# Retention with a two-layer MLP on one core: loads of tiles 18 to 23 in one run, v scaled by GpSimd alone, another order of late tasks

## The chip, the cores and the metric

The kernel runs on one core of one Trainium2 chip. The metric is the device time of one execution in microseconds (us). A core has engines that run side by side, each through its own list of instructions in order, and that wait for each other by semaphores: TensorE (PE; its weight loads are shown apart as PEld), VectorE (DVE), ScalarE (ACT), GpSimd (POOL) and SyncE (SP), which here only issues transfers. Transfers (DMA) are issued by SP, ACT and POOL and carried out by 16 DMA engines.

## The reference

Inputs q, k and v have the shape 4 x 8 x 768 x 64 (batch, heads, sequence, head width). The first half is a recurrent retention, the second a layer norm with a two-layer MLP and a residual:

```python
gamma = 1.0 - 2.0 ** (-5.0 - np.arange(H))
for t in range(S):
    state = gamma * state + np.einsum('bhd,bhe->bhde', k[:, :, t], v[:, :, t])
    y[:, :, t] = scale * np.einsum('bhd,bhde->bhe', q[:, :, t], state)
...
xn = (x - mu) / np.sqrt(var + 1e-06) * g_ln
ch = np.maximum(xn @ w_ch1, 0.0) @ w_ch2
return x + ch
```

x is y with its heads side by side, 3072 rows of 512; w_ch1 is 512 x 2048, w_ch2 is 2048 x 512. Inputs and output are fp32.

## The kernel before

The 3072 rows are cut into 24 tiles of 128 tokens. Tiles 0 to 3 are the first chunk of each batch; tiles 4 to 8 are chunks 1 to 5 of batch 0, 9 to 13 of batch 1, 14 to 18 of batch 2, 19 to 23 of batch 3. All matmuls are in bf16. Inside a chunk the recurrence is a masked product of scores; between chunks of a batch a state is carried on.

For each late tile (from tile 7 on) the steps are: POOL loads k, q and v (`k`, `q`, `v`, line 361, three DMAs of 128 KB with a cast to bf16) into ring buffers, eight slots for q with k and nine for v; SP transposes q and k together by DMA (`tr`, line 404); DVE scales the transposed q (`eq`, line 410); PE makes the scores of a pair of tiles in the four PSUM banks X0 to X3 and adds the carried state's part to the banks Y0 and Y1 (`vis`, lines 419 and 425); DVE applies mask and decay (`am`, line 432); PE multiplies by v (`py`, line 447). v scaled per head (`vg`) is made either by ACT in eight instructions, one for each head (line 478), or by POOL in one (line 481); PE multiplies it with k onto the bank PD, which sums over the chunks of a batch (`pd`, line 489), and DVE or ACT turns PD into the next state (`pb`, lines 500 and 504). There are three slots for scaled v, so a scaling waits until PE has used the one three chunks earlier.

The norm follows: DVE takes mean and variance (`bn`, lines 455 and 456), ACT the root (`sr`, line 586), DVE the reciprocal and the shift (`rt`, `nb`, lines 595 and 590), ACT copies y (`xc`, line 471) and normalizes it (`xg`, line 599), SP transposes it by DMA into `xnt` (`ex`, line 524). The first layer takes tiles in groups: eight of one tile, four of two (groups 8 to 11: tiles 8 and 9, up to 14 and 15), two of four (groups 12 and 13). `m8_4` is the block of group 8 that starts at hidden column block 4; it goes to one of the banks X0 to X3 (line 549), and ACT or DVE applies the relu into `h` and frees the bank (`r`, lines 560 and 562). Groups 12 and 13 use seven products instead of eight for a 2 x 2 block scheme (`f`, `fs`, `fo`, `fq`, `fr`, lines 670 to 711). The second layer runs tile by tile for tiles 0 to 7 (`z`, line 567) and in pairs with the seven products for the others (`s`, `sa`, `o`, lines 736, 725 and 750), and the result is stored (`st`, line 582).

**What sets the order.** Nothing is scheduled at run time: the list `ORDER` names every task in the order in which it is emitted, and each engine runs its own share of that list in order. `/A` behind a name puts it on ACT, `/D` or nothing on DVE (for `vg`, nothing means POOL), and the names behind `//` are the PSUM banks. A task on an engine that waits thus holds everything that stands behind it on that engine.

**The gates.** `gk17` and the like (`gate`, line 390) copy one element of a loaded buffer to `scrap` on POOL. They compute nothing: the copy waits for the landing of that load, and so POOL's later loads are issued only when it has landed. Landings are told on eight semaphores that POOL's loads use in turn (DMASW0 to DMASW7 in the rows below).

Of the kernel before, what the change touches and what calls it, by code (L numbers as in the profile page):

```python
# [52 lines left out]
am11a ad5 py10 r6_4/A py11 v14 pd11 m7_4//X1 bn11 pb12/A gq14 gk13 z6_0//M wg3/D st1/A gk15 r7_4/A
v13 pd12 bn10 m8_14//X0 sr11 xc11a q15 xc10b rt11 m8_8//X1 pb13 xc11b xc10a v15 sr10 nb11 z6_1 rt10
xg11b nb10 rs6 eq12 xg10b r8_14/A gk14 tr14 z6_2 wg1/D r8_8/A z6_3 v16 xg10a eq13 xg11a ex11/S
vis12//X0,X1,X2,X3 ad6 pd2 gv14 am13b vg14/ z7_0//M ex10/S pb14/A am12a m8_12//X3 gv13 am13a gq15
tr15 m8_2//X0 am12b tm4 py13 r8_2/A py12 z7_1 xc13a k16 xc13b bn12 r8_12/A pd14 m8_0//X0 vg15/A q16
bn13 z7_2 k17 sr13 m8_6//X1 xc12a rt13 q17 eq14 sr12 sq7 nb13 z7_3 rt12 pb15 xg13a v17 xg13b xc12b
m8_10//X2 ex13/S rs7 nb12 r8_6/A ad7 gv16 vg16/ r8_0/A m8_4//X1 r8_10/A gv15 xg12b k18 tm3 m9_8//X0
xg12a r8_4/A ex12/S pd15 st2/A eq15 s8_1//M r9_8/A sa8_1 st7/A gk17 vis14//X0,X1,X2,X3 pb16/A sa8_2  # L60
s8_5 gq17 am14a tr16 am14b pd16 gv17 m9_0//X0 gk16 am15a py14 am15b m9_4//X1 gk18 q20 py15 st3/A
m9_2//X2 tr17 bn15 r9_0/A k20 r9_4/A m9_6//X3 sa8_4 vg3/A q18 m10_2//X0 bn14 r9_6/A m9_12//X1 sa8_3
r9_2/A q19 sr14 s8_2//X3 sr15 r10_2/A o8_1 k19 xc15b vg17/A rt14 rt15 s8_6 nb15 pb17 gq20 s8_3 o8_2
r9_12/A eq16 xg15a m9_10//X0 xg15b o8_3 xc15a eq17 xc14b gq18 tr18 m9_14//X1 xc14a o8_4 v19 r9_10/A
nb14 wm3 xg14b s8_7 xg14a gq16 r9_14/A pd17 o8_5 vis16//X0,X1,X2,X3 pb18/A sa10_1 v18 tr19 s8_4
am16b gk19 am16a pd3 m10_4//X1 v20 ex15/S am17a py16 gq19 o8_6 st5/A m10_6//X0 ex14/S am17b st4/A
pb19/A bn16 s10_1//M tr20 py17 sa10_3 sr16 m10_10//X2 r10_6/A sa10_2 st6/A s10_5 rt16 r10_10/A
sa10_4 xc16b m10_12//X0 bn17 r10_4/A gv18 v21 m10_8//X1 wm1 sr17 gv19 xc17b k21 xc17a s10_2//X2
xc16a r10_8/A gk20 rt17 nb16 nb17 o10_1 m10_14//X3 r10_12/A vg20/ xg16b xg16a s10_6 xg17a q21 eq18
r10_14/A o10_2 s10_3 xg17b eq19 v22 vg19/A vis18//X0,X1,X2,X3 o10_3 o10_4 pd19 am19a s10_7 am18a  # L70
gk21 m10_0//X2 am18b q22 am19b m11_6//X0 k22 r10_0/A o10_5 pb20/A py18 sa12_1 q23 py19 s10_4 bn18
r11_6/A tr21 vg22/ pd20 m11_14//X0 o10_6 sr18 rt18 ex16/S vg21/ nb18 m11_0//X1 bn19 r11_14/A gv20
xc19b s12_1//M ex17/S gq21 eq20 r11_0/A wm2 sr19 s12_5 xg18b k23 xc18b pb21/A rt19 sa12_2 m11_8//X0
v23 nb19 sa12_3 xg19a m11_4//X1 xg18a o12_1 xg19b r11_8/A s12_2//X2 ex19/S sa12_4 xc19a r11_4/A wm4
pd21 s12_6 xc18a ex18/S pb22/A o12_2 s12_3 eq21 pd22 vis20//X0,X1,X2,X3 o12_3 tr22 o12_4 s12_7 am20a
pb23/A am21a f12_1_1//X0 am20b f12_0_1//PD m11_2//X2 xt12_1 fs12_0_1 am21b fs12_1_1 f12_0_5//X1
xt12_2 py20 tr23 o12_5 fs12_0_5 f12_0_2//X3 xt12_3 f12_0_6 r11_2/A fo12_0_1 py21 fs12_0_2 f12_0_3
bn20 f12_1_6 xc21a s12_4 st8/A fo12_0_2 fs12_1_2 f12_1_5//X2 xc21b xt12_4 xc20b f12_1_7 bn21
fs12_1_5 m11_10//X1 sr20 xc20a fo12_1_3 sr21 f12_1_3 r11_10/A rt20 rt21 m11_12//X3 nb20 nb21 eq23
xg20a eq22 f12_1_4 r11_12/A o12_6 f12_1_2//X1 fo12_1_2 xg20b f12_0_7 xg21b xg21a fo12_1_1 s14_1//M  # L80
fq12_1 ex21/S fo12_0_3 st13/A vis22//X0,X1,X2,X3 sa14_1 ex20/S f12_0_4 am23a s14_5 am23b f12_2_1//X2
am22b f12_3_1//X3 st9/A am22a py23 fs12_2_1 f12_2_5//X1 sa14_2 fs12_3_1 py22 f12_2_6 fs12_2_5 sa14_3
f12_3_6 fs12_2_2 sa14_4 f12_2_3 xc23a f12_3_5//X0 fs12_3_2 fo12_2_2 f12_2_7 fq12_0 o14_1 f12_3_7
st10/A f12_3_2//X1 xc22b bn22 fr12_0_1/A s14_6 fs12_3_5 bn23 s14_3 sr22 s14_2//PD rt22 sr23 o14_3
rt23 nb22 o14_4 f12_3_3 xg22b nb23 xg22a fo12_3_3 s14_7 xg23a ex22/S xc22a fo12_3_2 xg23b f12_3_4
xc23b o14_2 fr12_1_1/A f12_2_2//X0 o14_5 ex23/S f13_0_1//Y0 fr12_1_2/D fo12_2_1 s14_4 fo12_3_1
fs13_0_1 f13_0_2//X0 fo12_2_3 st11/A f13_2_1//X1 fq12_3 fo13_0_1 f13_1_1//Y1 fr12_2_1/A f12_2_4
# [763 lines left out]
```

## Time and profile before

| | |
|---|---|
| median of 3 runs | 207.77 us (207.06 to 208.0) |
| the profiled execution | 207.04 us |
| its span, first to last instruction | 205.2 us |
| granted TensorE clock | 0.998 |
| TensorE busy | 194.9 us, 95% |
| VectorE busy | 165.0 us, 80% |
| ScalarE busy | 126.0 us, 61% |
| GpSimd busy | 94.2 us, 46% |
| DMA queue of POOL's loads | 77024 packets, 13.37 MB |

Busy times are those of the engine's own instructions; issuing a DMA counts on POOL (some 0.9 us for each load) and not on SP or ACT. In groups of rows the columns are: line, engine, operation, output and inputs, shapes and count, then busy time, mean ns of one, and the idle time before them with what ended it. In timelines: start, duration, engine, line, operation, count, and in brackets the idle time of the engine just before, with what ended it. The end of the program is a run of PE products, a last addition and a store, in both versions the same.

### The profile page before, as it was taken

To read this page: it belongs to the slowest core of one execution; us is meant where nothing else is said; L and a number is where in the kernel's file an instruction comes from. 1 tells how busy PE (TensorE), PEld (TensorE's weight loads), DVE (VectorE), ACT (ScalarE), POOL (GpSimd) and SP (SyncE) were. 2 spreads that over 40 slices of the span, in tenths; PEclk is the share of its full clock that TensorE was granted. 3 is DMA by queue.
4 is the path that set the end of the run, shared out by engine and by line. 5 is a ranking of instruction groups with operands and counts; after the bars stand their busy time and mean duration, and the time that the engine had idled before them with its cause. 6 is when DMAs were issued, how large, how long until landed. Compare 5 with 4: busy or idle time off the path is not lost.

```text
span 205.2 us, 5787 instructions
## 1 busy us (share of the span) xinstructions
PE 194.9 (95%) x2292; PEld 159.3 (78%) x2303; DVE 165.0 (80%) x388; ACT 126.0 (61%) x316; POOL 94.2 (46%) x139
## 2 busy tenths in 40 slices
PE   7998999999999999998997998999999999999992
PEld 3568999897546576666986987988989888888881
DVE  6687899587258799967787996988988998879961
ACT  6376644641426998589499496895949896543000
POOL 8997593694597398695806198600000000000000
PEclk9999999999999999999999999999999999999999
DMA  8999999999999999999999999988142140102224
GB/s 128 173 182 180 159 194 167 175 181 156 159 111 166 147 118 168 169 155 209 179 133 107 205 190 104 137 75 126 56 144 65 26 131 0 51 3 102 104 82 177
DMA packets 110477, 27.16 MB, mean 132 GB/s; under 512 B 103153, under 2 KB 107505, under 8 KB 110450
## 3 DMA queue, kind: packets, MB, share of 16 engines
q0 software_dynamic: 77024, 13.37, 87.9%
q1 hardware_dynamic: 28770, 6.86, 24.4%
q10 hardware_dynamic: 4656, 6.56, 9.5%
q8 instruction: 18, 0.29, 0.6%
q14 instruction: 9, 0.07, 0.1%
HBM read 27.30 MB, written 6.29 MB: 164 GB/s over the span
## 4 chain that ended last, share of the span: by engine, by line
PE 37%; ACT 13%; DVE 3%; issue 2%; ACTq 0%; DVEq 0%
PE M L736 11%; PE X L670 8%; PE Y L736 5%; PE X L549 5%; ACT xn L599 3%; ACT vg L478 3%; ACT h L560 3%; PE Y L670 2%; PE PD L670 2%; ACT x_all L471 1%; PE X L736 1%; PE X L419 1%; PE Y L447 1%; ACT state L500 1%; PE PD L736 1%
## 5 line engine op out<-in xcount | busy, mean ns | idle before, releaser
L549 PE MATMUL X<-xnt,w 128*128 128x128 bf16 (+1 forms) x768 | 64.0, 237 | 0.9 <-ACT h L560 0.9
L549 PEld LDWEIGHTS <-w 128*128 128x128 bf16 x768 | 53.9, 98 | 6.0 <-issue 1.3
L560 ACT ACTIVATE h<-X 128x512 bf16<-128x512 f32 x57 | 33.5, 607 | 17.8 <-PE X L549 17.6
L432 DVE TENSOR_TENSOR asb<-X,mask 128x512 bf16<-128x512 f32 x48 | 30.3, 682 | 1.7 <-PE X L419 1.4
L736 PEld LDWEIGHTS <-h 128*128 128x128 bf16 x256 | 24.7, 98 | 3.3 <-issue 0.4
L567 PE MATMUL M<-w,h 128*128 128x512 bf16 x87 | 22.1, 379 | 0.5 <-issue 0.2
L567 PEld LDWEIGHTS <-h 128*128 128x128 bf16 x128 | 11.8, 98 | 11.7
L736 PEld LDWEIGHTS <-sum 128*128 128x128 bf16 x192 | 18.7, 98 | 2.6 <-issue 0.4
L455 DVE BATCH_NORM_STATS2 bns<-Y 128x6 f32<-128x256 f32 (+1 forms) x39 | 16.3, 451 | 5.2 <-PE Y L447 3.8
L471 ACT CAST x_all<-Y 128x256 bf16<-128x256 f32 (+1 forms) x39 | 14.8, 410 | 8.4 <-DVE xn L465 7.8
L361 POOL DMA_DIRECT2D v<-in_v_dram x20 | 17.8, 890 | 3.2 <-DMA w<-in_moe_w_ch_dram 2.2
L599 ACT ACTIVATE xn<-Y,shift,rstd 128x256 bf16<-128x256 f32 x32 | 16.7, 580 | 1.5 <-DVE shift L590 0.8
L361 POOL DMA_DIRECT2D qk<-in_k_dram x17 | 15.4, 906 | 1.0 <-issue 1.0
L361 POOL DMA_DIRECT2D qk<-in_q_dram x17 | 15.0, 889 | 1.1 <-issue 1.1
L500 ACT ACTIVATE state<-PD,gch 128x128 bf16<-128x128 f32 x40 | 11.7, 401 | 4.7 <-PE PD L489 3.6
L481 POOL TENSOR_TENSOR vg<-v,vsc 128x512 bf16<-128x512 bf16 x11 | 11.4, 1042 | 6.5 <-DMA v<-in_v_dram 6.5
L750 DVE TENSOR_TENSOR osb<-M,x_all 128x256 f32<-128x256 f32 (+1 forms) x18 | 9.1, 506 | 5.5 <-PE M L736 5.5
L390 POOL COPY scrap<-qk 1x1 bf16<-1x1 bf16 x28 | 8.9, 320 | 10.0 <-DMA qk<-in_q_dram 6.1
L736 PE MATMUL M<-early,sum 128*128 128x256 bf16 x96 | 12.4, 273 | 0.2 <-DVE osb L750 0.2
L736 PE MATMUL M<-w,h 128*128 128x256 bf16 x96 | 12.4, 273 | 0.0
L711 ACT ACTIVATE h<-h 128x1024 bf16<-128x1024 bf16 (+1 forms) x10 | 8.5, 862 | 5.5 <-DVE h L697 5.5
L725 DVE TENSOR_TENSOR sum<-h,sum 128x1024 bf16<-128x1024 bf16 x16 | 10.9, 681 | 0.1
(164 smaller groups left out, 375.6 us busy)
## 6 DMA issues: line engine op xcount, KB each, us to landing
out_dram<-osb ACTq DMA_DIRECT2D x23, 256.0 KB, 2.3
w<-in_moe_w_ch_dram POOLq DMA_DIRECT2D x8, 512.0 KB, 8.5
v<-in_v_dram POOLq DMA_DIRECT2D x20, 128.0 KB, 6.5
qk<-in_k_dram POOLq DMA_DIRECT2D x17, 128.0 KB, 6.6
qk<-in_q_dram POOLq DMA_DIRECT2D x17, 128.0 KB, 6.3
early<-in_q_dram POOLq DMA_DIRECT2D x6, 128.0 KB, 7.6
mid<-in_k_dram POOLq DMA_DIRECT2D x3, 128.0 KB, 6.8
mid<-in_v_dram POOLq DMA_DIRECT2D x3, 128.0 KB, 7.5
```

Source lines behind the costliest of these rows:

```text
L361: nc.gpsimd.dma_start(out=dst, in_=tok[kind][TILES[t]])
L432: nc.vector.tensor_tensor(out=slot(asb, t)[:, :, par, :], in0=bank(("pa", t, par)).rearrange("p (i t) -> p i t", t=P), in1=mask.rearrange( ...
L455: nc.vector.bn_stats(out=bns[:, t, i, :], in_=x)
L471: nc.scalar.copy(out=dst, in_=src)
L481: nc.gpsimd.tensor_tensor(out=slot(vgs, chunk(t)), in0=v_of(t), in1=vsc[:, c, :].unsqueeze(2).to_broadcast([P, H, D]), op=ALU.mult)
L500: nc.scalar.activation(out=slot(state, chunk(t) - 1)[:, i, :], in_=pd[:, i, :], func=AF.Copy, scale=gch[:, c - 1, i:i + 1])
L549: nc.tensor.matmul(bank(("mm", g, ho))[:, j * n * P:(j + 1) * n * P], lhsT=w1[:, ko, (ho + j) * P:(ho + j + 1) * P], rhs=x[:, x0:x0 + n, k ...
L560: nc.scalar.activation(out=dst, in_=src, func=AF.Relu)
L567: nc.tensor.matmul(bank(("m2", t)), lhsT=slot(h1, t // 4)[:, ho, t % 4 * P:(t % 4 + 1) * P], rhs=w2[:, ho, :], start=(ho == 0), stop=(ho = ...
L599: nc.scalar.activation(out=heads(slot(xns, t))[:, :, half], in_=split(y_of(t, half)), func=AF.Identity, bias=shift[:, t:t + 1], scale=rstd ...
L670: nc.tensor.matmul(f_bank(g, j, i)[:, n * w:(n + 1) * w], lhsT=f_left(i, ko)[:, (nb * j + n) * P:(nb * j + n + 1) * P], rhs=f_right(g, i)[ ...
L736: nc.tensor.matmul(product(t, i), lhsT=left(t, i)[:, ho, :], rhs=right[i][:, ho, :], start=(ho == 0 and i in (1, 2)), stop=(ho == HK - 1), ...
```

## The change

The list `ORDER` is replaced from the scores of tiles 8 and 9 on (some 62 us into the span), and nothing else. Its first lines:

```diff
-z2_3 ad0 tr10 gq10 z3_0//M v12 gk11 st0/A ad2 z3_1 tr11 eq8 q13 vis8//X2,X1,X3,X0 wg0/A tm1 z3_2
-am8a am8b z3_3 am9b pd9 am9a m7_12//X1 pb10/A gv10 gv11 ad3 q12 py8 py9 vg10/A z4_0//M bn9 z4_1 bn8
+z2_3 ad0 tr10 gq10 z3_0//M v12 gk11 st0/A ad2 z3_1 tr11 eq8 q13 vis8//X2,X1,X3,X0 wg0/A tm1 pd9 am8b
+z3_2 pb10/A am8a z3_3 am9a am9b m7_12//X1 gv10 q12 ad3 py8 py9 vg10/ z4_0//M bn9 z4_1 gv11 vg11/ bn8
...
```

Three things differ. Fifteen gates are gone: those of k of tiles 16 to 21, of q of tiles 16, 17, 18 and 20, of v of tiles 15, 16, 18, 19 and 20. The scaling of v of tiles 10, 11, 15, 3, 17 and 19, which was on ACT, is on POOL, so that none is left on ACT. And the late tasks stand in another order, with other banks; a few small tasks change between ACT and DVE (the first layer's weight scalings `wg1` and `wg2` and the states of tiles 14 and 17 change places; of the relus `fr` five go to DVE and three to ACT). No other task is added or removed: PE has the same 4605 rows.

On POOL, the place where the loads of tiles 18 to 20 begin. Before (`v_106` to `v_108` are slots of the v ring, `qk` the ring of q and k; what a row waits for stands in brackets, and a DMA row without brackets has had its waits fulfilled by rows ahead of it):

```order
L361 DMA qk_111<-in_q_dram 128x8x64 [waits DMAHW7_49]
L361 DMA qk_111<-in_k_dram 128x8x64
L361 DMA qk_111<-in_q_dram 128x8x64
L361 DMA qk_111<-in_q_dram 128x8x64 [waits DMAHW3_49,DMASW0_49]
L361 DMA qk_111<-in_k_dram 128x8x64
L390 COPY scrap_71<-qk_111 1x1 [waits DMASW5_49,Pool_49]
L390 COPY scrap_71<-qk_111 1x1 [waits DMASW7_49,Pool_49]
L361 DMA v6_108<-in_v_dram 128x8x64
L390 COPY scrap_71<-qk_111 1x1 [waits Pool_49]
L361 DMA v5_107<-in_v_dram 128x8x64
L390 COPY scrap_71<-qk_111 1x1 [waits DMASW1_49,Pool_49]
L361 DMA v7_109<-in_v_dram 128x8x64
```

and after the change, from v of tile 17 (`v4_106`) on:

```order
L361 DMA v4_106<-in_v_dram 128x8x64
L361 DMA qk_111<-in_q_dram 128x8x64 [waits DMAHW2_49]
L361 DMA qk_111<-in_k_dram 128x8x64
L361 DMA qk_111<-in_q_dram 128x8x64 [waits DMAHW3_49,DMASW6_49]
L481 TENSOR_TENSOR vg1_118<-v3_105,vsc_84 128x512 [waits PE_49]
L361 DMA v5_107<-in_v_dram 128x8x64 [waits DMASW7_49]
L361 DMA qk_111<-in_k_dram 128x8x64 [waits DMASW0_49]
L361 DMA v6_108<-in_v_dram 128x8x64 [waits DMASW1_49]
L390 COPY scrap_71<-v4_106 1x1 [waits DMASW3_49,Pool_49]
L361 DMA qk_111<-in_q_dram 128x8x64 [waits DMAHW7_49,DMASW2_49]
L361 DMA qk_111<-in_k_dram 128x8x64
L361 DMA qk_111<-in_k_dram 128x8x64 [waits DMAHW0_49,DMASW4_49]
```

The copies between the loads, which wait for landings, are gone but one, and the loads themselves carry the wait for the semaphore that a load eight places earlier uses; a scaling of v (`vg1_118`, tile 16) stands among them.

On ACT, between the first-layer blocks of group 9 (`h10`) ahead of the scores of tiles 16 and 17. Before, with the scalings of v of tiles 3 (`mid`) and 17 (`v4`):

```order
L560 ACTIVATE h10_129<-X0_61 128x2x256
L560 ACTIVATE h10_129<-X1_62 128x2x256
L478 ACTIVATE vg0_117<-mid_101,vsc_84 128x64 x8
L560 ACTIVATE h10_129<-X3_64 128x2x256
L560 ACTIVATE h10_129<-X2_63 128x2x256
L586 ACTIVATE rstd_91<-mv_90,epsb_76 128x1 x2
L560 ACTIVATE h11_130<-X0_61 128x2x256
L471 CAST x_all_96<-Y1_66 128x4x64
L478 ACTIVATE vg2_119<-v4_106,vsc_84 128x64 x8
L560 ACTIVATE h10_129<-X1_62 128x2x256
```

and after it, from an evacuation of the same group on:

```order
L560 ACTIVATE h10_129<-X0_61 128x2x256
L586 ACTIVATE rstd_91<-mv_90,epsb_76 128x1 x2
L560 ACTIVATE h10_129<-X3_64 128x2x256
L560 ACTIVATE h10_129<-X2_63 128x2x256
L560 ACTIVATE h10_129<-X1_62 128x2x256
L471 CAST x_all_96<-Y0_65 128x4x64
L560 ACTIVATE h11_130<-X0_61 128x2x256
L599 ACTIVATE xn3_125<-Y0_65,shift_92,rstd_91 128x4x64
L599 ACTIVATE xn2_124<-Y1_66,shift_92,rstd_91 128x4x64
```

The two times eight instructions of L478 are gone; evacuations (L560) and the norm's steps follow each other.

On SP, which issues all transposes: `tr` are q and k of a tile (L404), `xnt0` the normalized tiles 12 to 15, of which `xn2` is tile 14 and `xn3` tile 15, and `xnt1` tiles 16 to 19. The piece of the difference:

```order
 L524 DMA_TRANSPOSE xnt0_126<-xn1_123 128x4x128
-L524 DMA_TRANSPOSE xnt0_126<-xn0_122 128x4x128
+L404 DMA_TRANSPOSE tr_112<-qk_111 128x8x128 x2
+L524 DMA_TRANSPOSE xnt0_126<-xn3_125 128x4x128
 L404 DMA_TRANSPOSE tr_112<-qk_111 128x8x128 x4
-L524 DMA_TRANSPOSE xnt0_126<-xn3_125 128x4x128
 L524 DMA_TRANSPOSE xnt0_126<-xn2_124 128x4x128
-L404 DMA_TRANSPOSE tr_112<-qk_111 128x8x128 x2
+L404 DMA_TRANSPOSE tr_112<-qk_111 128x8x128
+L524 DMA_TRANSPOSE xnt1_127<-xn1_123 128x4x128
 L524 DMA_TRANSPOSE xnt1_127<-xn0_122 128x4x128
```

Tile 15's transpose (`xn3`) now stands ahead of those of q and k of tiles 18 to 21, and tile 14's (`xn2`) stays behind all four, where before only those of tiles 18 and 19 were ahead of both; behind tile 14 comes one `tr` (tile 23) in place of two.

More of the change, by code (lines that the diff above doesn't have):

```diff
@@ L53 @@
[L53 to L87, printed above, removed]
@@ new lines @@
+m10_8//X1 am16a pb19/A tr21 v23 bn17 m10_10//X3 r10_8/A vg20/ py16 ex14/S sr17 s10_1//M r10_10/A
+rt17 nb17 vg21/ bn16 s10_5 tr23 xc16a st6/A sr16 m10_4//X0 xc16b rt16 nb16 wm1 xg16a s10_2//X1
+r10_4/A xg16b m10_12//X3 xc17b o10_1 st7/A xg17b sa10_4 s10_6 xg17a r10_6/A ex17/S eq19 r10_12/A
+s10_3 eq18 xc17a o10_2 ex16/S vis18//X0,X1,X2,X3 o10_3 o10_4 pd19 am19b s10_7 pb20/A vg22/ am19a
+m10_0//X3 o10_5 gq21 am18a py19 r10_0/A s10_4 am18b sa12_1 pd20 py18 pb21/A m11_6//X0 o10_6 bn19
+m11_4//X1 bn18 sr19 pd21 s12_1//M r11_4/A sa12_2 sr18 s12_5 rt19 sa12_4 m11_14//X1 rt18 eq20 nb18
@@ new lines @@
+nb19 wm2 m11_8//X2 xg19a xg19b r11_6/A ex19/S m11_0//X3 xg18a o12_1 xg18b xc18a sa12_3 s12_2//X0
+xc19a ex18/S xc19b eq21 r11_14/A s12_6 o12_2 r11_0/A tr22 wm4 xc18b s12_3 r11_8/A pb22/A
+vis20//X0,X1,X2,X3 o12_3 o12_4 pd22 am20b s12_7 pb23/A am20a f12_1_1//X1 xt12_1 f12_0_2//X0 am21b
+fs12_1_1 py20 f12_0_1//PD xt12_2 st8/A am21a f12_1_5//X3 fs12_0_1 f12_1_6 xt12_3 py21 fo12_0_1
+fs12_1_2 f12_0_6 xt12_4 f12_0_5//X2 fs12_1_5 bn21 m11_2//X0 st11/A fs12_0_2 f12_1_3 bn20 fs12_0_5
+f12_1_7 r11_2/A f12_0_3 fo12_1_2 sr20 m11_10//X0 sr21 xc20b rt21 rt20 nb20 fo12_1_3 f12_0_7
@@ new lines @@
+f12_1_2//X3 nb21 o12_5 xg21b f12_1_4 fo12_0_3 xg20b r11_10/A s12_4 fo12_0_2 xg21a xg20a eq23
+m11_12//X0 xc21b ex20/S xc20a o12_6 fq12_1 fo12_1_1 f12_0_4 r11_12/A s14_1//M eq22 ex21/S xc21a
+sa14_1 fq12_0 vis22//X0,X1,X2,X3 sa14_2 f12_3_1//PD am23b s14_5 am23a f12_2_1//X3 am22b py23 st9/A
+f12_3_2//X2 am22a fs12_3_1 f12_3_5//X1 sa14_4 fs12_2_1 py22 f12_3_6 fs12_3_5 bn22 f12_2_6 xc22a
+s14_2//X0 fs12_3_2 bn23 sr22 fs12_2_2 f12_3_7 f12_3_3 xc22b o14_1 sr23 f12_2_7 rt22 o14_2 s14_6 rt23
+nb22 fo12_3_2 xg22a xg22b s14_3 nb23 xc23b fo12_3_3 ex22/S xg23b xg23a f12_2_5//X0 fo12_3_1 xc23a
@@ new lines @@
+s16_1//PD sa16_1 st15/A fr12_3_2/A f13_0_4 sa16_2 fs13_2_5 f13_2_7 fo13_1_2 s16_5 fs13_3_2
+f13_3_2//X0 fq13_0 o16_1 f13_2_3 fo13_3_1 f13_3_5//X2 f13_3_7 fo13_2_2 fs13_3_5 s16_2//X0 sa16_4
+s16_6 fo13_3_3 sa16_3 s16_3 fo13_2_3 f13_1_4 fr13_2_2/D f13_3_4 sa18_1 fq13_1 f13_2_4 o16_3 fq13_3
+s18_1//Y1 sa18_2 fr13_3_2/A o16_4 st14/A s18_5 o16_2 fr13_0_1/A sa18_4 f13_3_3 fr13_1_1/A fr13_2_1/D
+s16_7 fq13_2 s18_2//X0 o16_5 o18_1 s16_4 fo13_3_2 s18_6 fr13_3_1/D o16_6 s18_3 sa20_1 st17/A
+fr13_0_2/A sa20_2 s20_1//Y0 st16/A o18_3 s20_5 sa18_3 fr13_1_2/D s22_1//M o20_1 o18_4 s20_2//X1
@@ L100 @@
+sa20_4 s20_6 sa22_1 sa20_3 s22_5 o18_2 s22_2//X2 o22_1 sa22_2 s20_3 sa22_3 s18_7 o20_3 sa22_4 s22_6
+o18_5 o20_4 s22_3 s18_4 o22_3 o22_4 s20_7 o20_2 o22_2 s22_7 st22/A o20_5 o18_6 s20_4 st19/A o22_5
+st18/A s22_4 st20/A o20_6 st23b/A st21/A o22_6 st23a/A
 """.split()
```

38 lines of the change are left out of this document (23 added, 15 removed).

## The prediction

> **What bounds the kernel now.** I read the busy times first, then what TensorE (PE) waits for, then the rows at each wait.
>
> ```profile
> PE 194.9 (95%) x2292; PEld 159.3 (78%) x2303; DVE 165.0 (80%) x388; ACT 126.0 (61%) x316; POOL 94.2 (46%) x139
> PE X L419 <- ACT h L560: 1.2, 1, 1.2
> PE X L549 <- ACT h L560: 0.9, 1, 0.9
> PE PD L489 <- ACT vg L478: 0.5, 2, 0.3
> PE X L419 <- ACT h L702: 0.4, 1, 0.4
> PE M L736 <- DVE osb L750: 0.2, 1, 0.2
> PE PD L489 <- ACT state L500: 0.2, 1, 0.2
> ```
>
> The first row is the page's, the others are PE's waits from 62 us on (total, times, longest), without one of 0.2 us that names no engine. The order differs only from the scores of tiles 8 and 9 on, which PE starts at about 62 us; the matmuls are the same before and after, so the change can win PE's waits behind 62 us and no more. These seven waits are 3.4 us. The ends of matmuls are modelled, so each wait is longer than its row:
>
> ```profile
> L736 PE MATMUL M<-w,h 128*128 128x256 bf16 x96 | 12.4, 273 | 0.0
> 158.60 1.75 PE M L736 x16
> ```
>
> A 256-column matmul is shown 273 ns long (group row), but sixteen in a run take 1.75 us (chain), 109 ns each. The last one before a gap thus covers 0.16 us of it; seven gaps add 1.1 us. The **ceiling** of the gain is 4.5 us of PE's time.
>
> ```profile
> 93.89 1.91 PE L549 MATMUL X<-xnt,w 128*128 128x256 bf16 x16 [0.94 <-ACT h L560]
> 111.51 0.60 PE L419 MATMUL X<-trq,tr 64*128 64x128 bf16 x15 [1.18 <-ACT h L560]
> 122.12 1.03 PE L736 MATMUL M<-early,sum 128*128 128x256 bf16 x8 [0.24 <-DVE osb L750]
> 123.96 0.62 PE L419 MATMUL X<-trq,tr 64*128 64x128 bf16 x16
> 125.78 0.22 PE L489 MATMUL PD<-vg,qk 128*128 128x128 bf16 x1 [0.26 <-ACT vg L478]
> 138.48 0.38 PE L489 MATMUL PD<-vg,qk 128*128 128x128 bf16 x4 [0.22 <-ACT state L500]
> 151.50 0.62 PE L419 MATMUL X<-trq,tr 64*128 64x128 bf16 x16 [0.35 <-ACT h L702]
> ```
>
> These timeline rows place the waits (the scores of tiles 18 and 19, at 123.96, have none and are quoted for later); a twin of that at 125.78, 0.25 us, stands just before it. Five of the seven name ScalarE (ACT). What holds it there:
>
> ```profile
> 88.58 2.01 ACT L478 ACTIVATE vg<-v,vsc 128x64 bf16<-128x64 bf16 x8
> 101.63 1.77 ACT vg L478 x7
> 105.46 1.91 ACT vg L478 x8
> 123.72 2.02 ACT L478 ACTIVATE vg<-v,vsc 128x64 bf16<-128x64 bf16 x8
> sum 90.00, ACT 12.08; mean ACT 2.42
> ```
>
> Rows one and four are timeline, two and three the chain that ended last, five the sum of line 478 over windows from 62 to 152 us. Scaling v for one tile takes ACT eight instructions and 1.9 us; six tiles make 12.1 us. Each stands ahead of the evacuations (L560) that free score banks for PE.
>
> **The change, part by part.** *Scaling v on GpSimd (POOL).*
>
> ```profile
> L481 POOL TENSOR_TENSOR vg<-v,vsc 128x512 bf16<-128x512 bf16 x11 | 11.4, 1042 | 6.5 <-DMA v<-in_v_dram 6.5
> ```
>
> 48 ACT instructions go, POOL gets 6 x 1.04 = 6.3 us. At 93.89 ACT loses 1.9 us ahead of the wait, against 0.94 + 0.16; at 111.51 it loses 1.77 + 1.91 = 3.7 us, against 1.18 + 0.16; at 125.31 and 125.78 the waited-for work itself leaves, if POOL has it ready. I take these four waits as gone: 0.94 + 1.18 + 0.25 + 0.26 + 4 x 0.16 = 3.3 us. *Order:* the product on PD of tile 22 (138.48) is moved behind the scores of tiles 20 and 21, and one block (f12_0_4) ahead of the scores of tiles 22 and 23 is now followed by another product, so those two waits, 0.22 + 0.35 + 0.32 = 0.9 us, lose their cause too. The one at 122.12 belongs to POOL, below. The new order has its own tight places (four banks X0 to X3, each reused after two to four products). Unknown from the trace: at best nothing, at worst such waits as it shows at 93.89, 1.1 us; I take 0.4, as in the 138.48 row.
>
> *The port.* What VectorE (DVE) meets beside POOL's scaling:
>
> ```profile
> 120.33 1.13 DVE L590 SCALAR_TENSOR_TENSOR shift<-mv,rstd 128x1 f32<-128x1 f32 x2
> 120.34 1.03 POOL L481 TENSOR_TENSOR vg<-v,vsc 128x512 bf16<-128x512 bf16 x1
> 121.39 0.68 DVE L750 TENSOR_TENSOR osb<-M,x_all 128x512 f32<-128x512 f32 x1
> 90.89 1.02 DVE L410 TENSOR_TENSOR trq<-tr,qsc 128x512 bf16<-128x512 bf16 x1
> 128.41 0.95 DVE L725 TENSOR_TENSOR sum<-h 128x1024 bf16<-128x1024 bf16 x1 [0.75 <-ACT h L560]
> L590 DVE SCALAR_TENSOR_TENSOR shift<-mv,rstd 128x1 f32<-128x1 f32 x16 | 3.2, 209 | 0.1
> L410 DVE TENSOR_TENSOR trq<-tr,qsc 128x512 bf16<-128x512 bf16 x17 | 7.5, 447 | 3.1 <-DMA tr<-qk 3.0
> L725 DVE TENSOR_TENSOR sum<-h 128x1024 bf16<-128x1024 bf16 x8 | 5.7, 718 | 2.9 <-ACT h L560 2.9
> ```
>
> A 0.2 us shift pair took 1.13 us and ended with POOL's scaling; L410 took 1.02 instead of 0.45, L725 0.95 instead of 0.72, all beside it. Together about 1.7 us, over the seven scalings that POOL has behind 62 us: 0.25 us each. Six more cost DVE 1.5 us. The first case reached PE: the late osb at 121.39 is the wait at 122.12, 0.40 with its 0.16, so 0.4 of 0.9 us came through. I take 0.6 us of PE time for the six, within 0 (DVE has slack: 85% busy from 62 to 139 us) and 1.5 (all comes through), and keep the old 0.4 at 122.12 as not won. The Trainium skill speaks against the change here: in "SBUF — State Buffer", section "SBUF: two separate sides", the two engines share a port pair as an exclusive lock, and the second to come blocks fully. The trace agrees with that direction in the three rows above; what the rule would cost at its hardest is a rival below.
>
> *Loads.* Fifteen one-element copies (L390) go, with their waits.
>
> ```profile
> 105.22 0.18 POOL L390 COPY scrap<-qk 1x1 bf16<-1x1 bf16 x1 [3.21 <-DMA qk<-in_q_dram]
> 108.05 0.18 POOL L390 COPY scrap<-qk 1x1 bf16<-1x1 bf16 x1 [2.65 <-DMA qk<-in_q_dram]
> 117.17 0.57 POOL L390 COPY scrap<-v 1x1 bf16<-1x1 bf16 x1 [5.58 <-DMA v<-in_v_dram]
> v<-in_v_dram POOLq DMA_DIRECT2D x20, 128.0 KB, 6.5
> ```
>
> These three hold POOL for 11.4 us, yet no PE wait names a load. So I price earlier loads at nothing in themselves; what they buy is that PE, some 3 us earlier by then, still finds its tiles there. The landing waits are not all gone: by the order's rows a load now itself waits for the one eight before it, and a scaling queued behind such a load waits with it. That of tile 19 stands behind the loads of v and k of tile 22. PE needs it right behind the scores of tiles 18 and 19, 123.96 - 3 + 1 = 122 us.
>
> ```profile
> 89.58 0.91 POOL L361 DMA_DIRECT2D v<-in_v_dram  x1
> 130.52 0.89 POOL L361 DMA_DIRECT2D v<-in_v_dram  x1
> ```
>
> From v of tile 17 (first row) to v of tile 23 (second) before issued 18 more loads in 41 us, 2.3 us each with POOL's waits; issue alone is 0.9 us. I take 2.0. Three more scalings (3.1 us) stand ahead of the first row's load now, so it goes out at 90 to 93 us. The load that k of tile 22 waits for is the ninth behind it and lands by 90 + 18 + 6.5 = 114.5 to 117.5 us, so scaling 19 is ready by 118 to 121: hidden, by 1 to 4 us; without that cover each microsecond late is one of PE's.
>
> *SyncE (SP).* The transposes of q and k of tiles 18 to 21 and then that of normalized tile 14 now stand in a row.
>
> ```profile
> 110.88 5.01 SPq L524 DMA_TRANSPOSE xnt<-xn  x2
> 116.06 10.45 SPq L404 DMA_TRANSPOSE tr<-qk  x2
> DMA to landing us min/median/max: 2.4/3.4/8.8
> ```
>
> Before, tile 14 (second of the pair at 110.88) went out ahead of tiles 20 and 21; now behind both, so it needs q of tile 21, the tenth load behind v 17: 90 + 20 + 6.5 = 116.5 to 119.5 us. Then 1.3 us of issue and 3.4 (median of xnt, last row) to 8.8 us to land: 121 to 124, at worst 130. PE wants it for m11_6, three blocks of 0.87 us (8 of the 109 ns products) and some 0.7 us of small products behind 122: at 126. I take no wait; the bounds are 0 and 4 us, and the far end is a rival.
>
> *Sum:* won 3.3 + 0.9 = 4.2; paid 0.4 + 0.6 = 1.0; net 3.2 us. The profiled execution took 207.04 us (span 205.2 and 1.8 around it): 203.8 us. The median shown, 207.77, is 0.7 above it, and the same scatter may lie on the new one; it stands in the range, not in the forecast.
>
> **Rivals.** *Transposes late.* Loads now run beside all transposes, where POOL's waits left gaps before. For it: with a landing of 8.8 us, the longest quoted, tile 14 is up to 4 us late, and the scores of tiles 16 and 17 (111.51 before, 110 now) lose their spare time too. Against it: their scores, just as close in before, waited for ACT and never for a transpose. Price 1 to 2.5 us: 205.5. The Trainium skill, "DMA: Bandwidth & Descriptors", section "Queues, rings and completion order", has each engine go round its queues packet by packet, so that more loads waiting in one queue need not slow another; no run here shows that yet.
>
> *Slower by late loads.* q of tile 21 lands as late as before, since transfers and not POOL's waits set the pace. Before, SP's pair from 116.06, whose second is tile 21, ended at 126.5. Then tile 14 goes out at 126.5 and lands at 130 to 135, and PE, in order, stands at m11_6 from 126: 4 to 9 us lost against 3.2 won, 210.3 in the middle. It turns slower from a landing of q 21 at about 124. Against it: 11.4 us of POOL's waits leave the queue ahead of that load.
>
> *Slower by the port.* Each of the six scalings holds a DVE instruction for its whole length and PE waits for that instruction: 6 x 1.04 = 6.2 us, against 4.2 - 0.4 won: 209.4 us. The rows speak for one such hold in seven. This is the rule of "SBUF — State Buffer" in the Trainium skill at its hardest.
>
> *No effect.* ACT's freed time is eaten by the new order's bank waits, DVE's holds and a late transpose at their ends: 1.1 + 1.5 + 1 of 4.2 us, 206.4 us. Of this kind is also that the change does not do what it says: the loads still wait, eight apart, and go out no earlier.
>
> **How the numbers follow.** Forecast 203.8, its case from 202.5 (ceiling: 207.04 - 4.5) to 204.9, chance 0.50; late transposes, to 206.1, 0.24; no effect, to 207.8, 0.13; slower by late loads 0.09, by the port 0.04. A measurement here tells about 0.5%, 1 us, from no change. Faster takes the first case and most of the second: 0.71; same 0.15; slower 0.14. The range leaves out the slower cases and a piece of no effect: 202.4 to 206.9.
>
> **What would show it.** Right: no L478 group, PE's waits on ACT h gone near 93 and 110, the scores of tiles 18 and 19 near 121 and of 22 and 23 (151.50 before) near 148, at most six more stretched DVE instructions beside L481. Wrong: a PE wait at L549 for a DMA into xnt near 126, DVE trq (L410) waiting for tr, or PD (L489) waiting for POOL.

## The result, and the profile after

The changed kernel takes 213.78 us (median of 4 runs, 212.48 to 214.1) against 207.88 (207.06 to 209.08) for the kernel of before beside it: ratio 1.0267, interval 1.0201 to 1.0334. It is **slower by about 5.9 us**, where 3.2 us less were forecast. Ratios here leave disturbed runs out, so one can differ a little from the quotient of two medians. The profiled execution took 213.59 us, 6.55 more than the one of before.

Three rows of the page of after (busy time, mean of one, idle time before it):

```profile
PE 196.4 (93%) x2303; PEld 159.4 (75%) x2303; DVE 169.7 (80%) x390; ACT 113.9 (54%) x266; POOL 94.3 (45%) x130
L481 POOL TENSOR_TENSOR vg<-v,vsc 128x512 bf16<-128x512 bf16 x16 | 17.1, 1071 | 23.2 <-issue 12.2
L410 DVE TENSOR_TENSOR trq<-tr,qsc 128x512 bf16<-128x512 bf16 x17 | 8.6, 511 | 9.8 <-DMA tr<-qk 9.7
```

ACT lost the 12.1 us of scaling, as planned. But DVE's scaling of q (L410) now stands idle for 9.8 us over the whole run, 9.7 of it for transposes; before it was 3.1. From 62 us on, where the order differs, it waits three times for a transpose (first row below); before it had no such wait there. The other rows are PE's waits from 62 us on (total, times, longest):

```profile
DVE trq L410 <- DMA tr<-qk: 5.8, 3, 2.4
...
PE M L736 <- DVE osb L750: 3.3, 2, 1.9
PE X L549 <- DMA xnt<-xn: 2.2, 1, 2.2
PE X L419 <- DVE trq L410: 1.1, 1, 1.1
PE M L567 <- DVE osb L575: 0.7, 1, 0.7
PE X L419 <- ACT h L560: 0.4, 2, 0.3
PE PD L489 <- DVE state L504: 0.2, 1, 0.2
PE PD L489 <- ACT state L500: 0.2, 1, 0.2
PE X L549 <- DVE asb L432: 0.2, 1, 0.2
```

The waits on ACT fell from 3.0 us (L560, L702 and L478) to 0.4. New ones of 7.3 us (PE's first four rows) took their place. Where they stand in PE's timeline (start, length, idle time before):

```profile
86.66 0.40 PE L419 MATMUL X<-trq,tr 64*128 64x128 bf16 x8 [1.08 <-DVE trq L410]
109.31 1.09 PE L549 MATMUL X<-xnt,w 128*128 128x256 bf16 x8 [2.24 <-DMA xnt<-xn]
110.19 1.91 PE L736 MATMUL M<-early,sum 128*128 128x256 bf16 x8
111.90 1.85 PE L736 MATMUL M<-w,sum 128*128 128x256 bf16 x8
117.18 1.03 PE L736 MATMUL M<-w,h 128*128 128x256 bf16 x8 [1.46 <-DVE osb L750]
129.54 1.03 PE L736 MATMUL M<-early,sum 128*128 128x256 bf16 x8 [1.89 <-DVE osb L750]
131.38 0.62 PE L419 MATMUL X<-trq,tr 64*128 64x128 bf16 x16
157.96 0.62 PE L419 MATMUL X<-trq,tr 64*128 64x128 bf16 x16
```

The last two are the scores of tiles 18 and 19 and of 22 and 23: 7.4 and 6.5 us later than before. Behind the wait at 109.31 the same eight products take 1.91 and 1.85 us instead of 1.04. The windows of line 549 say why (window, length, PE and PEld busy, granted clock, DMA share, GB/s; the DMA share is the summed time of the packets over that of 16 engines, and can pass 1 because packets overlap):

```profile
110.00:112.00 2.00, 0.40 (x4) 0.06 (x1) 0.54 1.96 117
112.00:114.00 2.00, 0.18 (x2) 0.23 (x3) 0.61 3.10 147
```

The clock was granted at 0.54 and 0.61 on average (0.50 for 3.41 us from 110.15 on): 2 x 0.46 + 2 x 0.39 = 1.7 us of PE lost on top of the wait.

**Behind each of these four waits stands a transpose that landed late.** The transposes issued from 92 to 106 us of normalized tiles 12 and 13 (L524) and then of tiles 16 and 17 (L404), first before, then after, of tiles 16 and 17 only after (rows of the view of DMA: count, time of one issue, first and last start; time from issue to landing):

```profile
L524 SPq DMA_TRANSPOSE xnt<-xn x2: 1190/1190/1191, 93.1 to 95.7; - x2
...
DMA to landing us min/median/max: 3.4/3.6/3.9
...
L524 SPq DMA_TRANSPOSE xnt<-xn x2: 1694/2173/2652, 97.9 to 100.6; - x2
...
DMA to landing us min/median/max: 8.6/8.6/8.7
...
L404 SPq DMA_TRANSPOSE tr<-qk x2: 1406/3095/4784, 102.5 to 104.1; - x2
...
DMA to landing us min/median/max: 8.0/9.7/11.4
```

The second of normalized tiles 12 and 13, issued at 100.62, landed at 109.17: PE's wait at 109.31. Tile 17 landed after 11.4 us, at 115.47; before it took 8.8 us, to 107.59. Of these 7.9 us, 5.3 come from the later issue (104.11 for 98.77) and 2.5 from the slower landing; of normalized tile 13's 12.2 us (before: issued at 93.10, landed at 97.00) 7.5 and 4.7. Tile 13, issued at 75.76, after 10.4 us, at 86.16. DVE takes its tasks in order, so what stands behind the scaling of q waits too:

```profile
86.19 0.42 DVE L410 TENSOR_TENSOR trq<-tr,qsc 128x512 bf16<-128x512 bf16 x1 [2.04 <-DMA tr<-qk]
115.49 1.30 DVE L410 TENSOR_TENSOR trq<-tr,qsc 128x512 bf16<-128x512 bf16 x1 [1.27 <-DMA tr<-qk]
116.72 0.41 DVE L750 TENSOR_TENSOR osb<-M,osb 128x256 f32<-128x256 f32 x1
```

The first is PE's wait at 86.66; the third frees the bank that PE waits for at 117.18. In it the port has a share: L410 took 1.30 us instead of 0.45, beside POOL's scaling of tile 20 (115.44 to 116.50).

The wait at 129.54 goes through two more engines (timeline of SP, ACT and DVE):

```profile
115.52 11.46 SPq L404 DMA_TRANSPOSE tr<-qk  x4
126.55 0.34 ACTq L582 DMA_DIRECT2D out_dram<-osb  x1
126.93 0.29 ACT L586 ACTIVATE rstd<-mv,epsb 128x1 f32<-128x1 f32 x1 [2.79 <-DMA tr<-qk]
127.26 0.16 DVE L595 RECIPROCAL rstd<-rstd 128x1 f32<-128x1 f32 x1 [2.96 <-ACT rstd L586]
```

A store on ACT went out only when the transpose of tile 18 had landed (issued 115.52, landed 126.53): its issue waits for the semaphore that this transpose had used. The norm of tile 16 stood behind that store, DVE behind the norm, PE behind DVE. And the transposes of tiles 18 and 19 went out 7.4 us later than before (108.08), because in SP's line that of normalized tile 15, issued at 114.15, stands ahead of them now.

What ran beside them: packets by DMA queue from 98 to 104 us, before and then after, and from 114 to 118 us after (q0 carries POOL's loads, q1 the transposes; packets, MB, share):

```profile
q1 hardware_dynamic: 1822, 0.45, 76.3%
q0 software_dynamic: 1715, 0.22, 63.5%
...
q0 software_dynamic: 3418, 0.43, 121.1%
q1 hardware_dynamic: 514, 0.13, 20.4%
...
q0 software_dynamic: 4461, 0.56, 346.4%
q1 hardware_dynamic: 10, 0.00, 0.6%
```

From 98 to 104 us twice the load packets came with 28% of the transposes' packets. The transposes are not the same there (q and k of tiles 16 and 17 before, mostly normalized tiles 12 and 13 after), so the counts compare the traffic and not one transfer. From 114 to 118 us, in which those of normalized tile 15 and of tiles 18 and 19 were issued, ten packets of transposes went through. The prediction cited from the Trainium skill, "DMA: Bandwidth & Descriptors", section "Queues, rings and completion order", that each engine goes round its queues packet by packet, and took from it that a deep queue need not slow another: here it did. Whether the turns of the engines or the making of the transposes' packets held them, the rows don't tell.

Sum: the new costs are 2.24 + 1.7 (clock) + 1.46 + 1.89 + 1.08 + 0.72 (at 71.05, behind DVE's shift, 1.53 us beside the scalings of tiles 10 and 11) = 9.1 us; the waits on ACT give 2.6 back; 6.5 of the 6.55. Of these, 1.08 and 0.72 lie ahead of the run of loads, which begins at about 92 us. Later kernels that have the same order up to there show waits of PE between 62 and 92 us at other places, from 0.6 to 2.4 us in all, so these two are in part scatter between executions.

### The profile page after: what moved, and what is told of

It is laid out like the page before. It is cut to its first block, busy times and chain, and to the rows that moved or that the text cites. A ratio compares the mean times of both kernels' runs of the same rounds, so it can differ in the third digit from the quotient of the medians.

```text
span 211.8 us, 5731 instructions
## 1 busy us (share of the span) xinstructions
PE 196.4 (93%) x2303; PEld 159.4 (75%) x2303; DVE 169.7 (80%) x390; ACT 113.9 (54%) x266; POOL 94.3 (45%) x130
## 4 chain that ended last, share of the span: by engine, by line
PE 33%; DMA 9%; ACT 6%; DVE 4%; issue 1%; SPq 1%; ACTq 0%; DVEq 0%
PE M L736 8%; PE X L670 8%; DMA tr<-qk 5%; PE Y L736 5%; DMA xnt<-xn 4%; PE PD L736 2%; PE X L736 2%; PE X L549 2%; PE PD L670 2%; ACT h L560 2%; PE Y L670 2%; ACT xn L599 2%; DVE asb L432 1%; DVE osb L750 1%; ACT state L500 1%
## 5 line engine op out<-in xcount | busy, mean ns | idle before, releaser
L549 PE MATMUL X<-xnt,w 128*128 128x128 bf16 (+1 forms) x768 | 63.7, 237 | 2.4 <-DMA xnt<-xn 2.2
L549 PEld LDWEIGHTS <-w 128*128 128x128 bf16 x768 | 54.0, 98 | 7.5 <-issue 2.9
L560 ACT ACTIVATE h<-X 128x512 bf16<-128x512 f32 x57 | 33.5, 609 | 21.6 <-PE X L549 18.3
L481 POOL TENSOR_TENSOR vg<-v,vsc 128x512 bf16<-128x512 bf16 x16 | 17.1, 1071 | 23.2 <-issue 12.2
L567 PE MATMUL M<-w,h 128*128 128x512 bf16 x96 | 22.9, 379 | 0.7 <-DVE osb L575 0.7
L736 PEld LDWEIGHTS <-sum 128*128 128x128 bf16 x192 | 19.4, 102 | 5.0 <-issue 2.1
L410 DVE TENSOR_TENSOR trq<-tr,qsc 128x512 bf16<-128x512 bf16 x17 | 8.6, 511 | 9.8 <-DMA tr<-qk 9.7
L736 PE MATMUL M<-early,sum 128*128 128x256 bf16 x80 | 11.2, 287 | 1.9 <-DVE osb L750 1.9
L736 PE MATMUL M<-w,h 128*128 128x256 bf16 x80 | 10.4, 272 | 1.5 <-DVE osb L750 1.5
L750 DVE TENSOR_TENSOR osb<-M,x_all 128x256 f32<-128x256 f32 (+1 forms) x15 | 7.5, 503 | 3.3 <-PE M L736 3.1
L670 PEld LDWEIGHTS <-w 128*128 128x128 bf16 x96 | 9.2, 98 | 1.1
```

Of the source, the lines that this page charges most:

```text
L481: nc.gpsimd.tensor_tensor(out=slot(vgs, chunk(t)), in0=v_of(t), in1=vsc[:, c, :].unsqueeze(2).to_broadcast([P, H, D]), op=ALU.mult)
L549: nc.tensor.matmul(bank(("mm", g, ho))[:, j * n * P:(j + 1) * n * P], lhsT=w1[:, ko, (ho + j) * P:(ho + j + 1) * P], rhs=x[:, x0:x0 + n, k ...
L560: nc.scalar.activation(out=dst, in_=src, func=AF.Relu)
L567: nc.tensor.matmul(bank(("m2", t)), lhsT=slot(h1, t // 4)[:, ho, t % 4 * P:(t % 4 + 1) * P], rhs=w2[:, ho, :], start=(ho == 0), stop=(ho = ...
L670: nc.tensor.matmul(f_bank(g, j, i)[:, n * w:(n + 1) * w], lhsT=f_left(i, ko)[:, (nb * j + n) * P:(nb * j + n + 1) * P], rhs=f_right(g, i)[ ...
L736: nc.tensor.matmul(product(t, i), lhsT=left(t, i)[:, ho, :], rhs=right[i][:, ho, :], start=(ho == 0 and i in (1, 2)), stop=(ho == HK - 1), ...
```

## Experiments

Fifteen kernels. The edits are to `ORDER` (tasks `g..` are the waits for landings, `/A` puts a scaling on ACT).

**Parts of the change alone.** In the kernel of before without the fifteen waits:

```diff
-... gv16 gv15 gk17 gq17 gk16 gk18 gq20 gq18 gq16 gk19 gv18 gv19 gk20 gk21 gv20 ...
```

> The order of before without the fifteen gates, nothing else changed. Theory L (loads in one run crowd SyncE's transposes): 2 to 6 us slower than before, with transposes landing 8 to 11 us after their issue where they took at most 8.8, TensorE waiting on xnt or, over VectorE's trq, on tr. Theory P (GpSimd's scaling holds VectorE at the shared port) and theory O (the new order of late tasks is at fault by itself): within 1 us of before, about 207.

Measured: 208.95 us, ratio 1.0047 (1.0018 to 1.0076), about 1 us slower. Leaving out the waits alone is not the loss.

```diff
-vg10/A vg11/A vg15/A vg3/A vg17/A vg19/A
+vg10/ vg11/ vg15/ vg3/ vg17/ vg19/
```

> The order and gates of before, with only the scaling of v of tiles 10, 11, 15, 3, 17 and 19 moved from ScalarE to GpSimd. Theory P: 1 to 3 us slower than before, from stretched VectorE instructions beside L481. Theories L and O: 1 to 3 us faster, 204.5 to 206.5, since the four waits of TensorE behind ScalarE's scaling go (3.3 us at most).

Measured: 212.07 us, ratio 1.0185 (1.0128 to 1.0242), some 4 us slower, outside both expectations. Beside DVE (osb 2.1 us, trq 1.4), PE now waits for POOL's scaling: PD behind vg, 1.7 us. The scalings stand in POOL's line behind the waits for landings.

Both edits together:

> The order of before without the fifteen gates and with the six scalings on GpSimd: all of the change but its order of tasks. Theory O: faster than before or the same, 204.5 to 207.5. Theories L and P: slower, 209 to 213, close to the sum of the two runs that do one part each.

Measured: six runs from 204.83 to 212.15 us, median 208.55, between the two expectations; ratio 0.9886 (0.9834 to 0.9937). With such scatter I draw no verdict from it, but it is not 6 us slower. So the two edits together, in the order of before, are not the loss; that the scalings need the waits gone is suggested (212.07 against 208.55), not shown.

The changed kernel with its six scalings back on ACT:

> The changed kernel with the six scalings back on ScalarE. Theory P: 2 us or more faster than the changed kernel, below 211.6. Theory L: no faster, 213 to 215.5, with TensorE's waits on xnt and VectorE's on tr unchanged in size, since the loads still run in one piece.

Measured: 212.4 us, ratio 1.0232 (1.0189 to 1.0274), not told apart from the changed kernel's 1.0267. The loss stays when POOL has none of the six: the port is not the main part of it. PE's wait of 1.7 us at 107.69 is put down to ACT's vg, which those products don't read; it ended with the landing of a normalized tile at 107.56, so it is a late transpose again.

**Loads paced by waits.** A wait for the load three ahead, before each load from q of tile 18 on; then the same with the scalings on ACT:

```diff
-... q18 ... k18 ... q19 ...
+... gk17 q18 ... gq17 k18 ... gv17 q19 ...
```

> The changed kernel with waits put back among its loads: from q of tile 18 on GpSimd waits, before each load, for the landing of the load three ahead of it. Order and scaling as in the changed kernel. Theory C (crowding: the loads in one run slow the transposes beside them from some 4 us to 9 to 11 us, and PE waits for these): the waits of 2.2 us for xnt near 109 and of 1.5 us near 117, and the slow products behind the first, go; transposes of tiles 12, 13, 16, 17 land in 4 to 8 us; 208 to 210 us. Theory O (the new order itself needs its transposes too early): 212.5 to 215 us, with waits for DVE trq or xnt at the same places. If the waits make scalings and loads late instead: PD waiting for POOL or trq for tiles 18 to 21, 211 us or more.

> The same paced loads, and the six scalings on ACT: of the whole change only the order is left. Theory C: 206.5 to 208.5 us, since order alone costs next to nothing. Theory O: 211.5 to 213.5 us, as with scalings on ACT and loads in one run (212.4).

Measured: 215.62 us (ratio 1.0291, 1.0204 to 1.0378) and 215.59 (1.0343, 1.0251 to 1.0435). Both miss. The first kernel's waits of PE, the landings of tiles 16 and 17, and a scaling on POOL:

```profile
PE PD L495 <- POOL vg L487: 4.9, 2, 3.7
...
DMA to landing us min/median/max: 6.4/6.7/7.0
...
112.64 1.06 POOL L487 TENSOR_TENSOR vg<-v,vsc 128x512 bf16<-128x512 bf16 x1
```

The transposes do land sooner (6.4 and 7.0 us instead of 8.0 and 11.4), and PE's waits for them shrink from 2.24 and 1.46 us to 0.3 and none. But the scaling of tile 17 ran at 112.6 instead of 101.8, behind waits for landings, and PE waited 3.7 us for it. In the second kernel the two scalings took 4 us of ACT in one piece (107.23 to 111.18) ahead of evacuations, and PE waited 1.9 us there. The remedy cost what it cured, so these two don't tell the theories apart.

**SP's order.** The transposes of tiles 18 and 19 ahead of that of normalized tile 15:

```diff
-ex15/S ... tr18 ... tr19
+tr18 tr19 ex15/S
```

> The changed kernel with the transposes of q and k of tiles 18 and 19 issued ahead of that of normalized tile 15 on SP instead of behind it. If SP's order is what makes them late (part of theory O): both go out by 110 instead of 115.5 and 117.1, land by 121, the wait of 1.9 us near 129.5 goes, 211 to 212.5 us. Theory C: they go out earlier into the same crowd and take 10 us or more, the waits near 109 and 117 stay as they are, 213 to 214.5 us.

Measured: 211.67 us, ratio 1.0192 (1.013 to 1.0255), 2.1 us below the changed kernel. The wait near 129.5 is gone, as theory O said; those near 109 and 117 stay (1.3 us, ended by a landing at 108.79, and 2.6 us), as theory C said. The intervals of this kernel and the changed one overlap, so the 2.1 us rest on the wait that went and on a second pair below. SP's order is one cause, and not the only one.

**Loads in one run in the order of before.** First all, then only the twelve whose buffers are free, then these twelve behind the scaling of tile 16; all eighteen late waits for landings are left out, the fifteen and three more:

```diff
-... v17 ...
+... v17 q18 k18 q19 v18 k19 v19 q20 k20 k21 q21 v20 v21 ...
```

> The kernel of before without its waits, and with the loads of tiles 18 to 23 moved up in one run right behind v of tile 17, in the order of the changed kernel; all else in the order of before, scalings on ACT. Theory C: the transposes of normalized tiles 12, 13 and of tiles 16, 17 land in 7 to 11 us instead of 3.4 to 8.8, PE waits for xnt or trq between 95 and 115, 210 to 213 us. Theory O: as without the waits alone, 208.5 to 209.5 us, and no such PE wait over 1 us.

> The kernel of before without its waits, and only the twelve loads whose buffers are free moved up in one run behind v of tile 17, so that the scaling of tile 16 stands behind no load that waits. Crowding beside the order of before: its transposes of tiles 12, 13, 16, 17 land in 7 to 10 us as in the denser kernel; by the time PE had to spare there (3.6 us for tile 12, 7 for 16, 4 for 17) at most some 2 us come through: 208.5 to 211 us. If the loads in one run alone make the change slow: 212 us or more, with PE waits for xnt or trq above 2 us.

> The kernel of before without its waits, with twelve loads in one run, now right behind the scaling of tile 16 on GpSimd, so that only the transposes can suffer. If loads in one run are enough to make it slow in any order: transposes of tiles 16 to 19 land in 8 to 11 us and PE waits for them, 211 us or more. If they hurt only an order that leaves no spare time for transposes: those landings, but PE waits for DMA or trq under 1 us in all, 208 to 209.5 us.

Measured: 214.49 us (ratio 1.0301, 1.0217 to 1.0385), 212.78 (1.021, 1.0118 to 1.0303) and 209.6 (1.0066, 1.0027 to 1.0105). The first two lost their time otherwise than expected. PE's wait and POOL's line in the second:

```profile
PE PD L494 <- POOL vg L486: 7.0, 1, 7.0
...
103.19 0.87 POOL L366 DMA_DIRECT2D v<-in_v_dram  x1 [2.51 <-DMA v<-in_v_dram]
104.07 1.05 POOL L486 TENSOR_TENSOR vg<-v,vsc 128x512 bf16<-128x512 bf16 x1
```

The scaling of tile 16 stood behind the twelve issues, the last of which waited 2.5 us for a landing, and PE stood for 7 us behind it: a scaling in the line of the loads, not a transpose. The third kernel has that mended. Its landings of tiles 16, 17 and 19 (that of 18 the trace doesn't give), PE's wait and the DVE row behind it:

```profile
DMA to landing us min/median/max: 8.8/12.1/12.6
...
PE M L741 <- DVE osb L755: 2.7, 2, 1.9
...
107.64 0.69 DVE L755 TENSOR_TENSOR osb<-M,x_all 128x512 f32<-128x512 f32 x1 [3.31 <-DMA out_dram<-osb]
```

Transposes as late as in the changed kernel, but the order of before issues them early enough: PE waited 0.7 us for a normalized tile (ended by its landing at 103.55) and 0.8 us behind the scaling of q of tile 17. The longest, 1.9 us, came from a store of the output that landed late in the same crowd. So this kernel is 1.4 us slower than before; but the kernel of before with only the fifteen waits left out (1.0047) was already 1.0 us slower, and the two are not told apart. In the order of before, then, loads in one run cost some 0.4 us by these two kernels, which is not measurable; in the changed order they cost more, as the next two kernels measure.

**Loads later.** The changed kernel with loads moved behind scalings that wait for PE anyway, and two of its last three waits for landings (`gv17`, `gq19`) left out; then with the edit to SP's order too:

```diff
-q19 ... vg16/ ... v18 ... k19 ... v19 ... q20 ... k20 ... k21 ... vg17/ ... vg3/ ...
+q19 k19 ... vg16/ ... vg17/ ... vg3/ v19 q20 k20 v18 q21 k21 ... vg19/ v20 v21 q22 k22 ... vg20/ q23 k23 v22 ... vg21/ v23 ...
```

> The changed kernel with v of tile 18 and the loads of tiles 20 to 23 issued later, behind scalings that wait for PE anyway (tile 17 and 3: 6 loads; 19: 4; 20: 3; 21: 1), so that at most four loads are in flight beside the transposes of tiles 12, 13, 16 and 17, with no wait added. Order and scaling else as in the changed kernel. Theory C (crowding): these four transposes land in 4 to 7 us instead of 8.0 to 11.4; the waits of 2.2 us near 109 (with 1.7 us of slow products behind it) and 1.5 us near 117 go; 209 to 211 us; the wait near 129.5 may stay. Theory O (the order alone, whatever the loads): no faster than 213.

> The same later loads, and the transposes of tiles 18 and 19 ahead of that of normalized tile 15. If crowding and SP's order are the two causes, both gains add: 2 us from SP's order (213.8 to 211.7 measured) and 3 to 5 us from the loads: 207 to 209 us. If the two are one cause, no faster than the better of the two alone (about 211).

Measured side by side: 210.07 us (ratio 1.0124, 1.0051 to 1.0197) and 207.92 (1.0017, 0.9975 to 1.0059). The two gains add: by the medians 3.7 us from the loads and 2.1 from SP's order, 5.9 together. By the ratios, each to the kernel of before beside it, the loads give 1.4% and 1.75% (3.0 and 3.6 us, with SP's order unchanged and changed), SP's order 0.75% and 1.1% (1.6 and 2.2 us). In the first the wait of 2.24 us near 109 and the half clock behind it are gone, though its transposes of tiles 12, 13, 16 and 17 landed in 6.6 to 8.8 us and not in the 4 to 7 expected; waits of 1.6 us at 112.99, 1.7 at 125.16 and 1.4 at 133.70 are left. The landings of normalized tiles 12 and 13 in the second, and its longest wait:

```profile
DMA to landing us min/median/max: 6.2/6.8/7.4
...
PE M L741 <- DVE osb L755: 1.7, 1, 1.7
```

The longest, 1.7 us, is still behind the transpose of tile 17, which landed in 9.2 us with six loads in flight.

**Spread further, and the balance of POOL and ACT.**

```diff
-vg3/ v19 q20 k20 v18 q21 k21 ... vg19/ v20 v21 q22 k22 ... vg20/ q23 k23 v22 ... vg21/ v23
+vg3/ v19 q20 k20 ... vg19/ v18 q21 k21 v20 ... vg20/ v21 q22 k22 ... vg21/ q23 k23 v22 v23
```

> As with later loads and the transposes of tiles 18 and 19 first, but the loads spread more: three behind the scaling of tile 3, four behind that of 19, three behind 20, four behind 21. If what is left of crowding holds PE (1.7 us near 111.7, behind the transposes of tile 17 that landed in 9.2 us with 6 loads in flight): tile 17 lands in 6 to 8 us, that wait goes, 205.5 to 207 us, under the kernel of before. If something else of the change holds PE (port, bank waits of the order): 207.5 to 209 us as before this edit.

> The same, with the scalings of tiles 10, 11 and 15 back on ACT; those of 17, 3 and 19 stay on GpSimd and pace the loads. If the port matters here (DVE instructions held near 68, 73 and 84, each 0.4 to 0.8 us): 0.5 to 1.5 us less than with all six on GpSimd. If ACT was worth relieving there: 0.5 to 2 us more, with PE waits for ACT h near 72 and 94.

> The order of before without its waits, scalings of tiles 15, 3 and 17 on GpSimd, and the loads of tiles 18 to 23 spread behind scalings (2, 2, 4, 3, 2, 2, 3 at a time). If crowding and ACT's scalings were all that mattered: the waits for ACT h near 94 and 111.5 go (0.94 + 1.18 + 0.3 us), 205.5 to 206.5 us. If the port takes it back (DVE held beside the three scalings): 207 to 208.5 us. If a scaling again stands behind loads that wait: 209 us or more, PD waiting for POOL.

Measured: 207.31 us (ratio 0.9983, 0.9948 to 1.0018; one outlier of 335 us among 13 runs), 207.93 (0.9999, 0.9959 to 1.0039) and 208.49 (0.9984, 0.9946 to 1.0021). In the first the wait near 111.7 is gone, as expected (tile 17 in 7.1 us). None differs measurably from before, and putting three scalings back on ACT changes nothing measurable. PE's longest waits in the second of them:

```profile
PE X L424 <- ACT h L565: 0.6, 2, 0.4
PE M L572 <- DVE osb L580: 0.4, 2, 0.2
```

Its waits from 62 us on come to 2.0 us, and the profiled run took 206.44; but twelve runs spread from 206.4 to 214.0. In the third, the wait for ACT at 111.5 shrank to 0.2 us, and waits of 0.9 (state) and 0.8 us (asb) opened elsewhere. So no version was measurably faster than before, apart from the kernel with both edits, whose six runs scatter too much to tell.

**Landing against loads in flight.** Over the seventeen profiles from 62 us on, where the trace gives a landing, by the number of loads in flight when SP's issue of a transpose ended (issued and not yet landed; transposes issued one behind another add to the time):

| loads in flight | q and k of a tile: median us (count) | normalized tile |
|---|---|---|
| 0 | 3.6 (28) | 2.5 (125) |
| 1 to 2 | 5.9 (49) | 4.9 (50) |
| 3 to 4 | 7.4 (72) | 5.3 (55) |
| 5 to 6 | 9.2 (22) | 8.6 (14) |
| 7 to 8 | 10.1 (13) | 7.3 (6) |

## Why the prediction was wrong

*ACT's scaling: right in part.* The waits at 93.89, 111.51 and 125 are gone, and with 151.50's they are 3.0 us by their rows, of the 3.3 + 0.9 forecast. (Six of the seven waits listed name ACT, not five.) But moving the scalings is not what took all of them. In the order of before with the scalings on POOL, without and with the fifteen waits left out, the wait of 1.18 us shrank to 0.2 and those of PD for ACT's scaling went, yet that of L549 near 94 stayed: 0.5 us at 96.07 and 1.0 at 95.83. And in the changed order with the six scalings back on ACT, PE waited only 0.4 us for ACT h. So the new order has a part in it that the prediction gave to the scalings. The product on PD, forecast to wait no more, still waits for the state, 0.2 us at 145.82. *The order's own bank waits: right,* 0.4 us taken, 0.4 (ACT h) found; net, 2.6 us were won.

***Loads: the step that failed.*** "I price earlier loads at nothing in themselves": PE's waits in the profile of before named no load, so the transfers were free, and only their landing in time was checked. But the loads ran beside transposes whose landing PE does wait for, and the profile of before had the sign: 2.4 us at the shortest, 8.8 at the longest. In the changed order the earlier loads cost 3.0 to 3.7 us, which moving them later (with two waits for landings left out in the same edit) showed. In the order of before a run of loads cost no measurable time, although transposes landed as late: the cost is that of the crowd and of an order that leaves its transposes too little time (normalized tile 13 goes out 7.5 us later than before), together.

*Pace: wrong, without effect.* Two us a load were assumed. From v of tile 17 (91.93) to v of tile 23 (114.48) it was 22.55 / 18 = 1.25 us. The scaling of tile 19 was done by 112.8 (forecast 118 to 121), hidden as forecast, but by a pace that was wrong: that is luck. The faster pace is the crowd.

*SP: wrong place.* The prediction looked at normalized tile 14 behind tiles 18 to 21 and took no wait. That one went out at 127.08 and landed at 132.00, where 116.5 to 119.5 and 121 to 124 were forecast, and PE never waited for it, late as PE itself was by then: no wait was right by luck. (The forecast's own terms put PE's need at 122 + 2.6 + 0.7 = 125.3, not 126.) The step that cost was next to it: tiles 18 and 19 behind normalized tile 15, 1.6 to 2.2 us. That the landing of one transpose also holds a store on ACT, and so PE, was in none of the steps.

*Port: direction right, weight small.* 0.72 us at 71.05 and some of the 1.46 at 117.18 lie above the 0.6 taken. But with the six back on ACT the changed kernel is not measurably faster, nor the spread one with three. The rule of "SBUF — State Buffer" in the Trainium skill, section "SBUF: two separate sides", agrees with the stretched rows; the time doesn't hang on it.

*The rival "transposes late" was the mechanism,* held at 0.24 and priced at 1 to 2.5 us. It was mis-sized in three ways: landings up to 11.4 us instead of 8.8, waits at four places (tiles 13, 17, 18 and normalized 13) of which the rival named one, that of the scores of tiles 16 and 17, and the clock behind the longest. Of the signs named, L410 waiting for its transpose came; the wait of L549 for a transpose came at 109 and not near 126; PD never waited for POOL.

*The rest.* Mended in both places the change is level with before, not 3 us faster. In the profiled run with three scalings back on ACT, PE's waits from 62 us on are 2.0 us, against 3.4 before, and it took 206.44 us; the median over twelve runs shows no gain. Loads in flight still slow transposes there. What would have to go for 203.8 stays open.
